# A bank for each strand of side work, and an earlier turn for attention two batches ahead

## The chip, the cores and the metric

The kernel runs on one core of a Trainium2 chip. The metric is the device time of one execution in microseconds. The core's engines are PE (matrix multiply, with a weight load of its own, PEld), DVE (vector), ACT (activation), POOL (GpSimd) and SP, which here only issues DMAs. Each engine works through its own list of instructions in the order in which the program holds them, and semaphores make one engine wait for another.

## The reference, cut to what matters

Eight batches of 576 tokens with 8 heads of 64 go through three layers.

```
q_s = softmax(q, over features); k_s = softmax(k, over tokens)
kv  = k_s^T v             (64 x 64 per head)
x   = q_s kv              -> [8, 576, 512]
u   = x + real(fft over tokens and features of x)
un  = (u - mean) / sqrt(var + 1e-6)
y   = u + relu(un @ w_ch1) @ w_ch2          (512 -> 2048 -> 512)
xk, xr = mixes of y and of y one token earlier
k   = relu(xk @ w_k);  v = (k*k) @ w_v      (512 -> 1024 -> 512)
out = sigmoid(xr @ w_r) * v
```

All of it is float32 in and out. The kernel splits the large operands into two half-precision parts and multiplies three times instead of once.

## The kernel before, in words

The 4608 tokens are worked on in nine blocks of 512, while attention, the transform and their sums go by batches of 576. Block 1 needs all of batch 1 up to token 1023, so its norm needs the transform of batch 1; the norm of block 2 needs the transform of batch 2, and so on.

The feed-forward part (FFN) of a block runs over 16 steps f. `mm1(f)` is 12 matmuls (24 of half width in the first 8 steps of block 0) into one of two banks `h` (L940), then ACT and DVE make `hh` and `hl` of it (L945, L946). `mm2(f)` is 12 matmuls into the four banks `acc0` to `acc3` (L960). PSUM has eight banks: two `h`, four `acc` and two for everything else, the tag `side`.

Beside the FFN of a block runs the side work, in strands written as generators, of which `side()` takes steps at four places of each f. `front_x` is attention for batch after batch: the maxima (L303, L306, L311 to L315), the exponentials (L325, L332), the key-value product (L343, L344) with its scaling (L346 to L354), the transposes of q (L377, L381) emptied by ACT (L370), and the last product (L396) emptied by ACT into `u` (L397). It works in two halves of four heads per batch. `front_y` is the transform of a batch and the norm of the blocks that it completes. The transform forms sums and differences (L430, L441, L446), has a first stage of six groups of matmuls (L475, L478), each emptied by ACT (L482) and DVE (L485), a second stage of five groups (L495 to L499) emptied by L505, L508 and L509, and adds the result to `u` (L511 to L518). The norm makes the mean (L572 and L574 on POOL, L555 on PE, L584) and the variance (L586 and L587 on ACT, L590 and L591 on POOL, L555, L606, L607), a correction (L609 to L612), a product on POOL (L624) and the two halves of the next block's operand (L637 on ACT, L638 on DVE), which the first L940 of that block reads. `front_z` reads and splits the FFN's weights.

While block 0 runs, `side()` gives attention and the transform four turns each as long as attention of batch 1 is undone, then four turns to the transform alone until norm 1 is done. From block 1 on the two alternate.

Each use of a bank by the side work asks `aside` (beside the first batch, where the `acc` banks are free, it takes six banks in turn; later the two `side` banks in turn). A bank is given out again when the last reader of its earlier use is done. The program's order is not the order in which the generators run: a scheduler places the instructions of each engine by when it expects operands and banks to be ready, and then each engine keeps to that list.

After the FFN of block 8 a last part (L1003 to L1054) computes the third layer, with PE busy nearly throughout.

Of the kernel before, what the change touches and what calls it, by code (L numbers as in the profile page):

```python
# [21 lines left out]
NS = 290  # L22
# [21 lines left out]
def net(ctx, tc, q, k, v, w1, w2, mu_k, mu_r, w_k, w_v, w_r, ce_d, se_d, cs_d, ss_d, alt_d, id_d, out):  # L44
# [16 lines left out]

    turn_of = [0]

    def aside(first):

        if not first:
            return bank("side", 2)
        turn_of[0] += 1
        x = turn_of[0] % 6
        return bank("side", 2) if x in (0, 3) else bank(f"acc{(1, 2, 4, 5).index(x)}", 1)  # L70

    mm = nc.tensor.matmul

# [128 lines left out]
    def scales(w):  # L202


        ts = nc.vector.tensor_scalar
        m = wsc[:, 3 * w:3 * w + 1]
        inv = wsc[:, 3 * w + 1:3 * w + 2]
        mi, ii = m.bitcast(U32), inv.bitcast(U32)
        nc.vector.tensor_reduce(out=m, in_=amax[:, w, :], axis=AX.X, op=ALU.add)
        pt = aside(False)[:, 0:1]  # L210
        mm(out=pt, lhsT=one, rhs=m, start=True, stop=True)
        ts(out=inv, in0=pt, scalar1=2.0 ** -120, scalar2=None, op0=ALU.max)
        ts(out=mi, in0=ii, scalar1=1, scalar2=0x3F800000, op0=ALU.logical_shift_right, op1=ALU.bitwise_and)
        ts(out=ii, in0=mi, scalar1=0x7F800000, scalar2=None, op0=ALU.bitwise_xor)

        ts(out=inv, in0=inv, scalar1=(2.0 ** -55, 2.0 ** -51)[w], scalar2=None, op0=ALU.mult)
        ts(out=m, in0=m, scalar1=(2.0 ** 54, 2.0 ** 50)[w], scalar2=None, op0=ALU.mult)
        if w == 1:
            nc.vector.tensor_tensor(out=wsc[:, 6:7], in0=wsc[:, 0:1], in1=m, op=ALU.mult)
# [65 lines left out]
    def attention(b):  # L285
        tt = nc.vector.tensor_tensor
        for hf in range(2):
# [18 lines left out]
                tt(out=m[p, 2 * x:2 * x + 2, :], in0=m[p, 2 * x:2 * x + 2, :], in1=kt[p, 16:18, :], op=ALU.max)  # L306
            if b in MAX_PE:

                pt = aside(b == 0)
                for x in range(2):  # L310
                    nc.tensor.transpose(out=pt[:, 128 * x:128 * x + 128], in_=m[:, 2 * x:2 * x + 2, :], identity=ident)  # L311
                mx = wsc[:, 2:6:3, None]
                nc.vector.tensor_reduce(out=mx[:, :, 0], in_=pt[:, 0:256].rearrange("p (x c) -> p x c", x=2), axis=AX.X, op=ALU.max)
                for x in range(2):
                    mm(out=pt[:, 256 + 128 * x:384 + 128 * x], lhsT=mx[:, x].to_broadcast([128, 128]), rhs=ident, start=True, stop=True)  # L315
                m = pt[:, 256:512].rearrange("p (h d) -> p h d", h=4)
            else:
                nc.gpsimd.partition_all_reduce(out_ap=m, in_ap=m, channels=128, reduce_op=bass_isa.ReduceOp.max)
# [18 lines left out]
            beside = nc.gpsimd.tensor_tensor if (b, hf) in POOL_M else tt  # L337
            beside(out=qt, in0=qt, in1=st[:, 1].to_broadcast([128, 18, 64]), op=ALU.mult)
            yield 0
            kv = aside(b == 0)[:, 0:260].rearrange("p (a e) -> p a e", a=2)  # L340
            for x in range(2):
                for c in range(4):
                    mm(out=kv[:, x, :], lhsT=kc[:, c, 2 * x:2 * x + 2, :], rhs=vt[:, x, c, :], start=(c == 0), stop=False)  # L343
# [28 lines left out]
                    tt(out=dst(qTl), in0=src, in1=dst(qT).bitcast(F32), op=ALU.subtract)  # L372

            for x in range(2):
                pt = aside(b == 0)
                for c in range(4):
                    nc.tensor.transpose(out=pt[:, 128 * c:128 * c + 128], in_=qt[:, 4 * c + 2 * x:4 * c + 2 * x + 2, :], identity=ident)  # L377
                turned(lambda z: z[:, x, 0:512].rearrange("e (p c) -> e c p", c=4), pt.rearrange("e (c p) -> e c p", c=4))
                yield 1
            pt = aside(b == 0)  # L380
            nc.tensor.transpose(out=pt[:, 0:128], in_=qt[:, 16:18, :], identity=ident)  # L381
            turned(lambda z: z[:, :, 512:576], pt[:, 0:128].rearrange("e (x p) -> e x p", x=2))
            if (1, 0) < nxt < (B, 0):
# [5 lines left out]
                U[b] = up.tile([128, 4, S], F32, tag="u", name="u")  # L389
            for x in range(2):  # L390
                for h in range(2):
                    pt = aside(b == 0)
                    hs = slice(HALF * h, HALF * h + HALF)
                    parts = ((bdh, qT), (bdl, qT), (bdh, qTl)) if fx else ((bd, qT),)
                    for z, (a, c) in enumerate(parts):
                        mm(out=pt[:, 0:HALF], lhsT=a[:, x, 0:128], rhs=c[:, x, hs], start=(z == 0), stop=(z == len(parts) - 1))  # L396
                    ma = nc.scalar.activation(out=U[b][:, 2 * hf + x, hs], in_=pt[:, 0:HALF], func=AF.Copy)  # L397
                    if b == 0:
                        mark(hf, mv, ma)
                    yield 1  # L400
# [13 lines left out]
    def transform(b):  # L414
# [52 lines left out]
        for i in range(3):  # L467
            for e, (ch, cl, n0, n1) in enumerate(((ceh, cel, 0, NK), (seh, sel, NK, NK + 256))):
                j0, n = JT[e][i]
                js = slice(j0, j0 + n)  # L470
                pt = aside(b == 0)[0:n, 0:n1 - n0]
                first = True
                for g in range(2):
                    for a, c in ((eh, ch), (eh, cl), (el, ch)):
                        mm(out=pt, lhsT=a[:, e, g, js], rhs=c[:, g, :], start=first, stop=(e == 1 and g == 1 and a is el))  # L475
                        first = False
                if e == 0:
                    mm(out=pt, lhsT=x6[:, js], rhs=alt[:, 0:NK], start=False, stop=True)  # L478
# [10 lines left out]
        sd = fw.tile([128, 2, 2, NS], F32, tag="eo", name="sd")  # L489

        def stage2(cols, ch, cl):
            pt = aside(b == 0)[:, 0:NS]
            for i in range(2):
                for a, c in ((yh, ch), (yh, cl), (yl, ch)):
                    mm(out=pt, lhsT=a[:, i, cols], rhs=c[:, i, :], start=(i == 0 and c is ch and a is yh), stop=False)  # L495
            if ch is csh:
                mm(out=pt, lhsT=yh[0:64, 2, cols], rhs=cl[0:64, 2, :], start=False, stop=False)
            n = 128 if ch is csh else 96
            mm(out=pt, lhsT=yh[0:n, 2, cols], rhs=ch[0:n, 2, :], start=False, stop=True)  # L499
            return pt  # L500
# [49 lines left out]

    def mean(i, sq, cs, n):

        pt = aside(i == 0)
        if i < 2:
            mm(out=pt[:, 0:n], lhsT=ones, rhs=sq[:, 0, cs], start=True, stop=True)  # L555
        else:
            hl = hp.tile([128, 2, 512], F32R, tag="rs", name="hl", bufs=1)
            h, l = hl[:, 0, cs], hl[:, 1, cs]
            nc.scalar.activation(out=h, in_=sq[:, 0, cs], func=AF.Copy)
            nc.vector.tensor_tensor(out=l, in0=sq[:, 0, cs], in1=h.bitcast(F32), op=ALU.subtract)  # L560
            mm(out=pt[:, 0:n], lhsT=onesr, rhs=h, start=True, stop=False)
            mm(out=pt[:, 0:n], lhsT=onesr, rhs=l, start=False, stop=True)
        return pt

    def norm_part(i, sq, d, rs, c0, n):
# [7 lines left out]
        if not onpe:  # L573
            add(out=sq[:, 0, cs], in0=sq[:, 0, cs], in1=sq[:, 1, cs], op=ALU.add)  # L574
            yield 0
            yield 0
            pt = mean(i, sq, cs, n)
        else:
            pt = aside(i == 0)
            for b, s, m, o in segs:  # L580
                for t in range(4):
                    mm(out=pt[:, o - c0:o - c0 + m], lhsT=ones, rhs=U[b][:, t, s:s + m], start=(t == 0), stop=(t == 3))
# [6 lines left out]
        if not onpe:  # L589
            add(out=sq[:, 0:2, cs], in0=sq[:, 0:2, cs], in1=sq[:, 2:4, cs], op=ALU.add)  # L590
            add(out=sq[:, 0, cs], in0=sq[:, 0, cs], in1=sq[:, 1, cs], op=ALU.add)  # L591
            yield 0
            yield 0
            pt = mean(i, sq, cs, n)
        else:
            pt = aside(i == 0)
            for t in range(4):
                mp = mm(out=pt[:, 0:n], lhsT=ones, rhs=sq[:, t, cs], start=(t == 0), stop=(t == 3))
            if i == 0:
                mark(5, mv, ma, mp)  # L600
# [49 lines left out]
    def everywhere(x, n):  # L650

        dg = W["pool"].tile([128, 4, 128], F32, tag="dg", name="dg", bufs=1)[:, 0:n]
        nc.vector.tensor_tensor(out=dg, in0=W["ident"][:, None, :].to_broadcast([128, n, 128]), in1=x[:, :, None].to_broadcast([128, n, 128]), op=ALU.mult)
        pt = bank("side", 2)[:, 0:128 * n]
        mm(out=pt, lhsT=ones, rhs=dg.rearrange("p x c -> p (x c)"), start=True, stop=True)
        nc.vector.tensor_reduce(out=x, in_=pt.rearrange("p (x c) -> p x c", c=128), axis=AX.X, op=ALU.max)
        nc.vector.tensor_scalar(out=x, in0=x, scalar1=float(DM), scalar2=None, op0=ALU.mult)
# [132 lines left out]
    def token_scale(i):  # L790


        n = blocks[i][1]
        pt = bank("side", 2)
        mm(out=pt[:, 0:n], lhsT=W["onesb"], rhs=SQ[i][:, 0:n], start=True, stop=True)
        rg = W["pool"].tile([128, 2, 512], U32, tag="rg", name="rg", bufs=2)
        rb = W["pool"].tile([128, 512], BF16, tag="rb", name="rb", bufs=1)
# [5 lines left out]
    def token_descale(i, rb, subs):  # L803

        z = SC[i][0]
        pt = bank("side", 2)
        for x, (o, m) in enumerate(subs):
            mm(out=pt[0:m, x:x + 1], lhsT=rb[:, o:o + m], rhs=W["onesb"][:, 0:1], start=True, stop=True)
        dd = W["pool"].tile([128, 2, 4], F32, tag="dd", name="dd", bufs=2)
# [358 lines left out]
```

## Time and profile before

| | |
|---|---|
| time, median of 3 runs | 1575.92 us (1575.87 to 1577.27) |
| profiled execution, its own time | 1579.14 us |
| its span, first to last instruction | 1577.2 us |
| granted clock of PE, mean | 0.964 |
| PE busy, share of the span | 93% |
| DVE, ACT, POOL | 59%, 41%, 15% |

A row of a timeline begins with the start in us from the span's start and the duration in us; what follows is the engine, the line of the kernel, the operation, the tile written and the tiles read. In brackets stands how long the engine had been idle and what released it. Matmuls follow each other faster than their duration says, since they are pipelined. A granted clock of 1.00 is 2.4 GHz and one of 0.50 is 1.2 GHz.

### The profile page before, as it was taken

How to read it: one execution, taken by the hardware profiler on the slowest of the kernel's cores; microseconds unless marked ns; L12 is line 12 of the kernel's file. 1: busy time of each engine (PE TensorE's matmuls, PEld its weight loads, DVE VectorE, ACT ScalarE, POOL GpSimd, SP SyncE). 2: the span in 40 equal slices, each digit the busy share in tenths (PEclk: the TensorE clock that was granted, in tenths of full speed). 3: DMA queues.
4: the chain of work that ended last, by engine and by line, in shares of the span. 5: the costliest groups of instructions: out<-in, count | busy, mean ns of one | idle time of the engine just before them, and what ended most of it. 6: DMA issues, size and time to landing. Idle time of an engine off the chain costs nothing. (4 is left out here: it accounts for less than half of the span.)

```text
span 1577.2 us, 18465 instructions
## 1 busy us (share of the span) xinstructions
PE 1459.6 (93%) x7135; PEld 760.4 (48%) x7135; DVE 927.9 (59%) x1629; ACT 651.2 (41%) x1183; POOL 237.9 (15%) x183
## 2 busy tenths in 40 slices
PE   4537998996999999999989989999999999999999
PEld 4425654553555555655545434444444444444444
DVE  7895726648648547556553581686785456554423
ACT  5676513423323233233232441463665445544322
POOL 1663502002010020020010120232010000000000
PEclk9767999997999999999999999999999999999999
DMA  8641102202102102111110540331111011100000
GB/s 308 193 142 47 48 0 75 79 16 74 48 0 74 47 1 74 48 35 43 44 54 1 193 169 1 100 114 64 57 54 54 1 54 54 54 1 27 27 27 27
DMA packets 43988, 99.81 MB, mean 63 GB/s; under 512 B 5723, under 2 KB 12156, under 8 KB 43900
## 3 DMA queue, kind: packets, MB, share of 16 engines
q1 hardware_dynamic: 43900, 98.63, 18.2%
q8 instruction: 56, 0.92, 0.2%
q14 instruction: 32, 0.26, 0.1%
HBM read 79.73 MB, written 18.87 MB: 63 GB/s over the span
## 5 line engine op out<-in xcount | busy, mean ns | idle before, releaser
L940 PE MATMUL h<-unh,wr 128*128 128x512 f16 (+1 forms) x1216 | 378.2, 375 | 38.3 <-ACT unh L637 26.3
L960 PE MATMUL acc<-hh,wr 128*128 128x512 f16 x1152 | 367.0, 381 | 3.9 <-ACT hh L945 3.9
L940 PEld LDWEIGHTS <-wr 128*128 128x128 f16 x1824 | 177.9, 99 | 239.3 <-issue 32.4
L960 PEld LDWEIGHTS <-wr 128*128 128x128 f16 x1728 | 166.3, 98 | 205.4 <-issue 15.1
L940 PE MATMUL h<-unl,wr 128*128 128x512 f16 (+1 forms) x608 | 227.1, 374 | 2.7 <-DVE unl L638 2.5
L960 PE MATMUL acc<-hl,wr 128*128 128x512 f16 x576 | 219.5, 381 | 4.3 <-DVE hl L946 4.3
L946 DVE SCALAR_TENSOR_TENSOR hl<-h,hh 128x512 f16<-128x512 f32 x144 | 98.7, 687 | 161.8 <-ACT hh L945 161.1
L1031 PE MATMUL acc<-wvh,kke 128*128 128x512 f16 x576 | 181.5, 379 | 0.0
L1016 PE MATMUL h<-x,wkh 128*128 128x512 f16 x576 | 171.3, 379 | 0.0
L945 ACT ACTIVATE hh<-h 128x512 f16<-128x512 f32 x144 | 84.5, 590 | 193.0 <-PE h L940 192.9
L1031 PEld LDWEIGHTS <-kke 128*128 128x128 f16 x864 | 84.5, 98 | 102.0
L1021 ACT ACTIVATE kke<-kke 128x512 f32<-128x512 f32 x72 | 45.1, 626 | 164.1 <-DVE kke L1020 164.0
L1020 DVE SCALAR_TENSOR_TENSOR kke<-h,rg 128x512 f32<-128x512 f32 x72 | 49.6, 688 | 102.5 <-PE h L1016 102.4
L1031 PE MATMUL acc<-wvl,kke 128*128 128x512 f16 x288 | 109.2, 379 | 0.0
L1016 PE MATMUL h<-x,wkl 128*128 128x512 f16 x288 | 109.2, 379 | 0.0
L1003 PE MATMUL h<-wrh,x 128*128 128x512 f16 x288 | 88.4, 379 | 1.6 <-ACT kke L1004 1.6
L1016 PEld LDWEIGHTS <-wkh 128*128 128x128 f16 x576 | 55.8, 98 | 66.0
L1023 DVE TENSOR_TENSOR kke<-kke 128x512 f16<-128x512 f32 x72 | 49.6, 689 | 61.0 <-ACT kke L1022 60.5
L572 POOL TENSOR_TENSOR sq<-u 128x128 f32<-128x128 f32 (+7 forms) x15 | 26.4, 1758 | 300.2 <-DVE u L517 133.7
L1003 PEld LDWEIGHTS <-x 128*128 128x128 f16 x432 | 42.3, 98 | 53.3 <-issue 3.0
L780 DVE SCALAR_TENSOR_TENSOR aa<-y,ms,aa 128x512 f32<-128x512 f32 x72 | 62.2, 872 | 4.8 <-ACT aa L776 3.0
L781 ACT ACTIVATE x<-aa 128x512 f16<-128x512 f32 x72 | 44.1, 621 | 35.9 <-PE h L1016 19.0
(322 smaller groups left out, 2170.1 us busy)
## 6 DMA issues: line engine op xcount, KB each, us to landing
vt<-in_v_dram SPq DMA_DIRECT2D x16, 650.0 KB, 5.0
kt<-in_k_dram SPq DMA_DIRECT2D x16, 576.0 KB, 3.8
qt<-in_q_dram SPq DMA_DIRECT2D x16, 576.0 KB, 3.7
out_dram<-oo SPq DMA_DIRECT2D x36, 256.0 KB, 2.1
y<-yT SPq DMA_DIRECT2D x8, 1026.0 KB, 4.9
raw<-in_w_dram SPq DMA_DIRECT2D x16, 512.0 KB, 4.4
words<-in_w_dram SPq DMA_DIRECT2D x16, 512.0 KB, 4.3
raw<-in_w_k_dram SPq DMA_DIRECT2D x32, 256.0 KB, 4.0
```

Source lines behind the costliest of these rows:

```text
L780: nc.vector.scalar_tensor_tensor(out=a, in0=y[:, t, 1:n + 1], scalar=mu[:, w, 0, t:t + 1], in1=a, op0=ALU.mult, op1=ALU.add)
L781: nc.scalar.activation(out=h[:, t, 0:n], in_=a, func=AF.Copy)
L940: mm(out=pt[:, o:o + m], lhsT=a, rhs=c[:, t, o:o + m], start=(t == z == 0), stop=(t == 3 and z == 2))
L945: nc.scalar.activation(out=hh[:, 0:n], in_=pt[:, 0:n], func=AF.Relu)
L946: nc.vector.scalar_tensor_tensor(out=hl[:, 0:n], in0=pt[:, 0:n], scalar=0.0, in1=hh[:, 0:n], op0=ALU.max, op1=ALU.subtract)
L960: mm(out=acc[x][:, 0:n], lhsT=a, rhs=c[:, 0:n], start=(f == z == 0), stop=(f == NF - 1 and z == 2))
L1003: mm(out=pt[0:m, :], lhsT=a[:, t, o:o + m], rhs=c[:, t, :], start=(t == 0 and a is rh and c is wrh), stop=(t == 3 and a is rl))
L1016: mm(out=pt[:, 0:n], lhsT=a[:, t, fs], rhs=c[:, t, 0:n], start=(t == 0 and a is wkh and c is kh), stop=(t == 3 and a is wkl))
L1020: nc.vector.scalar_tensor_tensor(out=kr[:, 0:n], in0=pt[:, 0:n], scalar=0.0, in1=G[:, 0:n], op0=ALU.max, op1=ALU.mult)
L1021: nc.scalar.activation(out=kr[:, 0:n], in_=kr[:, 0:n], func=AF.Square, scale=2.0 ** -76)
L1023: nc.vector.tensor_tensor(out=l2[:, 0:n], in0=kr[:, 0:n], in1=h2[:, 0:n], op=ALU.subtract)
L1031: mm(out=acc[x][0:m, :], lhsT=a[:, o:o + m], rhs=c[:, f, :], start=(f == 0 and a is h2 and c is wvh), stop=(f == NFK - 1 and a is l2))
```

## The change

`aside` takes the strand as a second argument. Strand 0, which is attention and the weights' scale, uses a tag `side0` with one bank; strand 1, which is the transform and the norm, a tag `side1` with one bank. The two banks are the two that `side` had. In the last part the two sums over tokens each get one of the two. And in block 0, once attention of batch 1 is done and until norm 1 is done, attention (of batch 2) gets the third of four turns.

```diff
-    def aside(first):
+    def aside(first, strand):
 
         if not first:
-            return bank("side", 2)
+            return bank(f"side{strand}", 1)
         turn_of[0] += 1
         x = turn_of[0] % 6
-        return bank("side", 2) if x in (0, 3) else bank(f"acc{(1, 2, 4, 5).index(x)}", 1)
+        return bank(f"side{x // 3}", 1) if x in (0, 3) else bank(f"acc{(1, 2, 4, 5).index(x)}", 1)
...
-            kv = aside(b == 0)[:, 0:260].rearrange("p (a e) -> p a e", a=2)
+            kv = aside(b == 0, 0)[:, 0:260].rearrange("p (a e) -> p a e", a=2)
...
-                pt = aside(b == 0)[0:n, 0:n1 - n0]
+                pt = aside(b == 0, 1)[0:n, 0:n1 - n0]
...
-            turns = (sx, sy) * 4 if done_att[0] < 1 else (sy,) * 4 if done_norm[0] < 1 else (sx, sy) * 2
+            turns = (sx, sy) * 4 if done_att[0] < 1 else (sy, sy, sx, sy) if done_norm[0] < 1 else (sx, sy) * 2
```

On PE before, the first group of the first stage of transform 1 stands in the middle of block 0, between FFN matmuls:

```order
L475 MATMUL side<-ceh,eh 128x258
L475 MATMUL side<-cel,eh 128x258
L475 MATMUL side<-ceh,el 128x258
L478 MATMUL side<-alt,x_97 128x258
L940 LDWEIGHTS wr
L940 MATMUL h<-unh,wr 128x512
L960 LDWEIGHTS wr
L960 MATMUL acc_777<-hh,wr 128x512
```

On PE after, the end of the same group, with its numbers of tiles (`side_1053` and `side_1067` are two uses of `side1`), stands at the last FFN matmul of block 0, the L960 here:

```order
L475 MATMUL side_1053<-ceh,el 128x258
L478 MATMUL side_1053<-alt,x_97 128x258
L960 LDWEIGHTS wr
L960 MATMUL acc_780<-hh,wr 128x512
L475 MATMUL side_1067<-seh,eh 128x256
L475 MATMUL side_1067<-sel,eh 128x256
```

What follows it, five groups of the first stage and the whole second stage, moved from the middle of block 0 to behind its end.

The first mean of norm 1 on PE before has FFN matmuls of block 0 on both sides:

```order
L960 LDWEIGHTS wr
L960 MATMUL acc_777<-hh,wr 128x512
L555 MATMUL side<-sq,onesr 128x512
L960 LDWEIGHTS wr
L960 MATMUL acc_777<-hl,wr 128x512
```

The same on PE after, with the variance's L555 six rows later (`kvbd_99` belongs to the second half of a batch, here batch 2):

```order
L396 MATMUL side_1451<-qT,kvbd_99 128x288
L555 MATMUL side_1258<-sq,onesr 128x512
L343 MATMUL side_1528<-vt,kt 128x130 x4
L344 MATMUL side_1528<-vt,kt 128x130
L343 MATMUL side_1528<-vt,kt 128x130 x4
L344 MATMUL side_1528<-vt,kt 128x130
L555 MATMUL side_1280<-sq,onesr 128x512
L377 MATMUL side_1561<-ident,qt 128x128 x4
```

All of this stands after block 0's last FFN matmul and before block 1's first; the last L396 of batch 2 and the key-value product of batch 3 are now around the norm's two products.

On DVE before, from the norm's correction to the first two halves of the operand of block 1:

```order
L609 TENSOR_TENSOR rs<-rs 128x512
L610 SCALAR_TENSOR_TENSOR rs<-side,rs 128x512
L346 TENSOR_SCALAR rk<-side 128x2
L611 TENSOR_SCALAR rs<-rs 128x512
L347 RECIPROCAL rk<-rk 128x2
L612 TENSOR_TENSOR rs<-rs 128x512
L352 TENSOR_TENSOR kvbd_98<-side,rk 64x2x64 x2
L303 TENSOR_REDUCE m<-kt 128x256
L306 TENSOR_TENSOR m<-m,kt 64x128 x2
L638 TENSOR_TENSOR unl<-d,unh 128x512 x2
```

On DVE after, the same place:

```order
L328 TENSOR_TENSOR kt<-kt,m 128x1024
L331 TENSOR_TENSOR kt<-kt,m 64x128 x2
L609 TENSOR_TENSOR rs<-rs 128x512
L610 SCALAR_TENSOR_TENSOR rs<-side_1280,rs 128x512
L611 TENSOR_SCALAR rs<-rs 128x512
L612 TENSOR_TENSOR rs<-rs 128x512
L485 TENSOR_TENSOR yl<-side_1550,yh 128x258
L638 TENSOR_TENSOR unl<-d,unh 128x512
L322 TENSOR_REDUCE st<-qt 128x18
L638 TENSOR_TENSOR unl<-d,unh 128x512
L485 TENSOR_TENSOR yl<-side_1567,yh 128x256
L324 TENSOR_TENSOR qt<-qt,st 128x1152
```

The attention here is that of batch 3 instead of batch 2, and steps of transform 2 stand between the four L638.

## Rows read from the trace of the kernel before

**Rows 1.** The page, busy us, share of the span, instructions of each engine.
```profile
PE 1459.6 (93%) x7135; PEld 760.4 (48%) x7135; DVE 927.9 (59%) x1629; ACT 651.2 (41%) x1183; POOL 237.9 (15%) x183
```
**Rows 2.** The waits of PE: us in total, times, longest us.
```profile
PE h L940 <- ACT unh L637: 26.3, 3, 17.1
```
**Rows 3.** Windows: length, busy us (instructions) by engine, PEclk, DMA share, GB/s.
```profile
119.00:245.40 126.40, 116.54 (x653) 72.77 (x652) 66.21 (x109) 59.17 (x104) 36.72 (x29) 0.93 0.08 31
245.40:258.80 13.40, 7.16 (x38) 4.96 (x38) 6.63 (x12) 5.16 (x9) 8.65 (x5) 0.94 0.58 209
258.80:366.50 107.70, 107.68 (x547) 59.37 (x545) 60.98 (x105) 35.84 (x64) 8.83 (x6) 0.99 0.11 35
366.50:384.40 17.90, 7.92 (x45) 6.70 (x44) 17.03 (x24) 6.48 (x15) 6.76 (x3) 0.69 0.46 163
384.40:394.00 9.60, 7.04 (x17) 2.36 (x17) 9.49 (x13) 4.32 (x7) 1.46 (x2) 0.51 0.00 1
700.00:720.00 20.00, 17.37 (x89) 9.57 (x88) 18.84 (x32) 7.32 (x13) 2.38 (x2) 0.91 0.46 146
816.00:824.00 8.00, 4.33 (x13) 1.87 (x13) 7.91 (x12) 3.65 (x7) 2.53 (x2) 0.57 0.42 142
```
**Rows 4.** Timeline of PE at the starts of blocks 1 and 2.
```profile
249.73 1.06 PE L343 MATMUL side<-vt,kt 128*128 128x130 f32 x8
...
258.83 1.06 PE L940 MATMUL h<-unh,wr 128*128 128x512 f16 x2
...
384.43 1.01 PE L940 MATMUL h<-unh,wr 128*128 128x512 f16 x2 [6.76 <-ACT unh L637]
...
394.04 0.38 PE L940 MATMUL h<-unl,wr 128*128 128x512 f16 x1
394.25 0.59 PE L940 MATMUL h<-unh,wr 128*128 128x512 f16 x2
```
**Rows 5.** Timeline of transform 1 in block 0, its groups and their emptying.
```profile
199.69 0.47 PE L475 MATMUL side<-seh,eh 128*128 128x256 f32 x1
...
201.72 0.39 PE L940 MATMUL h<-unh,wr 128*128 128x512 f16 x1
...
201.82 0.39 ACT L482 ACTIVATE yh<-side 128x258 fp32r<-128x258 f32 x1 [0.65 <-PE side L478]
...
202.24 0.43 DVE L485 TENSOR_TENSOR yl<-side,yh 128x258 fp32r<-128x258 f32 x1 [0.61 <-ACT yh L482]
...
212.86 0.30 PE L495 MATMUL side<-csh,yh 128*128 128x290 f32 x1
...
214.32 0.39 PE L940 MATMUL h<-unh,wr 128*128 128x512 f16 x1
...
218.46 0.48 PE L495 MATMUL side<-ssh,yh 128*128 128x290 f32 x1
...
219.59 0.30 PE L495 MATMUL side<-csh,yh 128*128 128x290 f32 x1
```
**Rows 6.** Timeline of norm 1 and of block 0's end, three engines.
```profile
230.57 0.75 DVE L518 TENSOR_TENSOR u<-u,sd 128x574 f32<-128x574 f32 x1
...
233.55 1.26 POOL L574 TENSOR_TENSOR sq<-sq 128x512 f32<-128x512 f32 x1
...
239.45 1.02 PE L555 MATMUL side<-sq,onesr 128*128 128x512 f32 x2
...
243.53 2.72 DVE L978 SCALAR_TENSOR_TENSOR u<-acc,wsc,u 128x512 f32<-128x512 f32 x4 [0.67 <-PE acc L960]
...
254.00 4.68 POOL L624 TENSOR_TENSOR d<-d,rs 128x1024 f32<-128x1024 f32 x2 [3.29 <-DVE rs L612]
```
**Rows 7.** DVE by line: count, busy us, mean ns, idle before, releaser.
```profile
L303 DVE TENSOR_REDUCE m<-kt 128x256 f32<-128x1024 f32 x16 | 31.0, 1936 | 15.0 <-DMA kt<-in_k_dram 15.0
L334 DVE TENSOR_REDUCE st<-qt 128x18 f32<-128x1152 f32 x16 | 21.6, 1349 | 7.4 <-ACT qt L325 7.4
L328 DVE TENSOR_TENSOR kt<-kt,m 128x1024 f32<-128x1024 f32 x10 | 12.2, 1222 | 1.6 <-POOL m L318 1.6
```

More of the change, by code (lines that the diff above doesn't have):

```diff
@@ L209, in scales @@
         nc.vector.tensor_reduce(out=m, in_=amax[:, w, :], axis=AX.X, op=ALU.add)
-        pt = aside(False)[:, 0:1]
+        pt = aside(False, 0)[:, 0:1]
         mm(out=pt, lhsT=one, rhs=m, start=True, stop=True)
@@ L307, in attention @@
             if b in MAX_PE:
-                pt = aside(b == 0)
+                pt = aside(b == 0, 0)
                 for x in range(2):
@@ L374, in attention @@
             for x in range(2):
-                pt = aside(b == 0)
+                pt = aside(b == 0, 0)
                 for c in range(4):
@@ L379, in attention @@
                 yield 1
-            pt = aside(b == 0)
+            pt = aside(b == 0, 0)
             nc.tensor.transpose(out=pt[:, 0:128], in_=qt[:, 16:18, :], identity=ident)
@@ L391, in attention @@
                 for h in range(2):
-                    pt = aside(b == 0)
+                    pt = aside(b == 0, 0)
                     hs = slice(HALF * h, HALF * h + HALF)
@@ L491, in stage2 @@
         def stage2(cols, ch, cl):
-            pt = aside(b == 0)[:, 0:NS]
+            pt = aside(b == 0, 1)[:, 0:NS]
             for i in range(2):
@@ L551, in mean @@
     def mean(i, sq, cs, n):
-        pt = aside(i == 0)
+        pt = aside(i == 0, 1)
         if i < 2:
@@ L578, in norm_part @@
         else:
-            pt = aside(i == 0)
+            pt = aside(i == 0, 1)
             for b, s, m, o in segs:
@@ L595, in norm_part @@
         else:
-            pt = aside(i == 0)
+            pt = aside(i == 0, 1)
             for t in range(4):
@@ L653, in everywhere @@
         nc.vector.tensor_tensor(out=dg, in0=W["ident"][:, None, :].to_broadcast([128, n, 128]), in1=x[:, :, None].to_broadcast([128, n, 128]), op=ALU.mult)
-        pt = bank("side", 2)[:, 0:128 * n]
+        pt = bank("side0", 1)[:, 0:128 * n]
         mm(out=pt, lhsT=ones, rhs=dg.rearrange("p x c -> p (x c)"), start=True, stop=True)
@@ L793, in token_scale @@
         n = blocks[i][1]
-        pt = bank("side", 2)
+        pt = bank("side0", 1)
         mm(out=pt[:, 0:n], lhsT=W["onesb"], rhs=SQ[i][:, 0:n], start=True, stop=True)
@@ L805, in token_descale @@
         z = SC[i][0]
-        pt = bank("side", 2)
+        pt = bank("side1", 1)
         for x, (o, m) in enumerate(subs):
```

## The prediction

> **What bounds the kernel now.** I read the page first, then the waits of PE, then windows cut at the ends of the feed-forward (FFN) blocks, then the timeline at those ends. The page shows PE busy for 93% of the span [rows 1], so time is lost only where PE stands still or runs at half speed. The waits say where: the largest releaser of PE is L637, the first operand of the next block, three times, 17.1 us of them at the start of block 0 and the rest at later block starts [rows 2]. The windows give the price of the starts [rows 3]. Inside block 0 PE is busy for 116.5 of 126.4 us and inside block 1 for 107.68 of 107.70, although the side work (attention, transform, norm) runs there: beside FFN matmuls it costs PE its own time and no waiting. Between block 0 and block 1, from 245.4 to 258.8, PE is busy for 7.2 of 13.4 us. Between block 1 and block 2 PE is busy for 7.9 of 17.9 us, and then runs 9.6 us at a granted clock of 0.51, the 1.2 GHz level. Two smaller places follow, at 700 to 720 and 816 to 824. So what counts is how much of the norm that a block needs is still undone when the FFN matmuls of the block before run out.
>
> **What the change adds: the transform of batch 1 loses its cover.** The program holds as many instructions on PE, DVE, ACT and SP after as before; all is order. With one bank, every step of attention waits until ACT or DVE has emptied the step before, and the order places these steps some 21 FFN matmuls apart. Attention of batch 1 now ends near the end of block 0 instead of half way. The order shows the consequence. Before, the first stage of transform 1 (L475), its second stage (L495) and the first mean (L555) stood among the FFN matmuls of block 0. After, only the first of six L475 groups does; then block 0's last matmul is issued, and five L475 groups, all of L495 and both L555 follow, with attention of batch 2, half of batch 3 and two groups of transform 2 between them, and no FFN matmul before L940 of block 1, which needs the norm. I work out the length of this uncovered stretch, counted from block 0's last FFN matmul.
>
> First the chain alone. A pair of L475 groups takes 2.03 us on PE (199.69 to 201.72), and the bank is free after L482 (0.39) and L485 (0.43) [rows 5]: with one bank a group costs 1.0 + 0.95, near 2.0 us, and five cost 10. Stage two has csh groups of 1.46 us (212.86 to 214.32) and ssh groups of 1.13 (218.46 to 219.59) [rows 5]; with their evacuation in series, and the four additions to u behind them, I take 12.6. The norm took from the end of L518 (231.3) to the end of the first of two L624, which together are 4.68 (256.3), and 0.6 for L637: 25.6 us, in which L555 stood ready at 234.8 and started at 239.45 [rows 6]: 21.0 without that wait. Before the chain moves, DVE has the four L978, L328 and L331 in front of the first L485: 3. Sum 46.6 us.
>
> Then what stands in the way. DVE is in order, and its list from block 0's last L946 to the first L638 grows from 10 to 59 us when each instruction is priced at its mean: three L303 (1.94 each), three L322 and three L334 (1.35), four L328 (1.22) and the tail [rows 7]. Some 3 us of it are done before the block ends, so 56 is a floor unless instructions overlap. Step by step along the queues I find these delays on the chain: 1.3 for the key-value product of batch 2 (two runs of eight L343 of 1.06 each, with L344 some 2.4 us on PE [rows 4]) in front of the third L475 group; 2.0 for an L303 that waits for its keys (its group waited 15.0 us on that DMA in all [rows 7]) in front of an L485; 1 and 1.4 for L396, L381 and L311 in front of groups; 1.7 to 3.6 for the second key-value product in front of the last ssh group; 1.7 for L370 in front of L515; 2 for L322, L430 and L324 in front of L584; 6 for the 17 us of DVE work between L584 and L609, more than ACT, POOL and PE take there. Sum 17 to 19, so 64 to 65 us. If PE runs at the lower level throughout, its groups take up to twice as long and the sum is 73. Here PE is busy for about half the time, and in 366.5 to 394 it ran at 0.69 and then 0.51 in such a state [rows 3]; I take the middle, 69.
>
> Its end is not clean either: behind the first L638 stand L322, L485 and L324 before the last L638, so the first L940 group ends 3.8 us late, and 1.5 more go in the return to full speed. So 74 us pass. In them PE does useful work that it would have done anyway: transform 1 (5.0 + 6.6), two L555 (2.0), two groups of transform 2 (2.0), and three times what the stretch 245.4 to 258.8 holds without its L555 (7.16 - 1.0, at full speed near 5.8, [rows 3]), with 0.4 for L311 and L315: 33. **Added: 74 - 33 = 41 us.** Bounds: 56 with the same tail, less 33, is 27; 73 and 9 more for DVE slowed beside POOL is 54.
>
> The Trainium skill has a rule against this change: "Perfetto Trace Analysis", Matmuls, says that independent groups should rotate through several banks, so that emptying one overlaps the next group's matmuls. The trace agrees in the price of a handover, 0.95 us behind a group [rows 5], and by that rule alone eleven groups of transform 1 would lose some 10 us; in the sum above these are in the 10 and the 12.6.
>
> The skill's "TensorE: Matmul & The Clock Gate", HAM oscillation, says that waits between bursts of matmuls throttle PE and the next burst starts slow. The rows 366.5 to 394 agree [rows 3]; by it the stretch would be 73 and the added part 45, without it 64 and 36.
>
> **What the change removes.** The old gap between block 0 and 1: 13.4 us with 6.1 us of useful work at full speed, and 1.3 in a slow start: 8.6 [rows 3, 4]. The gap between block 1 and 2: from 366.5 to 394.0 only 19 FFN matmuls were done (4.1 us at the spacing of 394.04 to 394.25) and side work that is busy for 7.9, some 6.1 at full speed: 17.3 [rows 3, 4]. It goes, since norm 2 stands in block 1's first half after the change (its last L562 halfway through, before the last L562 stood behind block 1's matmuls). What is late next there is nothing that I see: L624 of norm 2 is issued some three f steps early. The two later places are 3.5 and 5.2 us [rows 3]; norm 6 moves ahead of its block's end in the order, the other place I cannot tell: 5 of 8.7. **Removed: 8.6 + 17.3 + 5 = 31 us**, bounds 26 and 37 (all of 8.7, and 2.5 for a wait in block 0). The rest costs nothing: after block 5 both orders have the same norms at the same rows, and the tail is PE bound.
>
> Sum: 41 - 31 = **10 us slower**; 1589 against the profiled execution's 1579.1 (span 1577.2 and 1.9 around it), and 1586 against the median of 1575.9, which lies 3.2 lower. A measurement of this kernel tells 0.2%, 3.2 us, from no change. From the bounds: 27 - 37 = -10 to 54 - 26 = +28, so 1566 to 1604.
>
> **Rivals.**
> *The head start wins.* The stretch is bound by DVE's list alone and that is shorter than its means: four L978 in a row took 2.72 [rows 6], where four means of 0.744 make 2.98, and at that ratio the list of 56 comes to 51. Then 51 + 3.8 - 33 = 22 is added, 37 removed: -15, 1561. For it: PE and ACT work there is interleaved just so that the banks alternate, and block 1 starts with attention 2 done. Against: the chain has waits for keys and two PE queues in it. It decides from a stretch under some 56 us to L940, or under 62 if all 37 are removed.
> *The single bank stalls PE inside the blocks too.* PE is in order; where a bank is not emptied when the next side group is due, FFN matmuls wait behind it. After block 0 attention makes about 130 handovers; at 0.2 us each that is 26, 1612. For it: nothing can overtake on PE. Against: the order puts 4.5 us of FFN between handovers, and PE stood busy through block 1 [rows 3].
> *It comes out even*, within 3 us: a stretch of 56 to 62 us with 31 removed, or the bank split does nothing, as there are two side banks before and after. Against the latter: the order, in which the split doubles the length of attention 1.
>
> **Chances.** Forecast, +3 to +28: 0.58. Stalls in the blocks, or a stretch over 82: 0.10. Even: 0.08. Head start wins: 0.24. So slower 0.68, same 0.08, faster 0.24. The forecast's own range is 1579 to 1604; with 0.03 left out above and the reach into the faster side, 1564 to 1607.
>
> **What would show it.** In the profile after: a stretch of 60 to 80 us with no L940 or L960 near 232 to 305, PE about half busy at a clock of 0.5 to 0.8 in it; L940 released by L637 or L638 at its end; no gap of over 3 us between blocks 1 and 2; PE without waits inside block 1. If block 1 starts before 290, or L377 and L396 wait inside blocks, or the gap between block 1 and 2 stays, a step is wrong.

## The result

The changed kernel takes 1597.37 us (median; 1595.03 to 1597.77), the kernel before 1576.16 in the same comparison: +21.2 us, a ratio of 1.0130 [1.0114, 1.0146]. The forecast was +10. The profiled execution of after is the fastest of its runs (1595.03, span 1593.2), that of before the slowest of its own (1579.14): between the two traces 16.0 us of span are to be explained.

The page and the waits of PE after, which answer to [rows 1, 2]:

```profile
PE 1465.1 (92%) x7135; PEld 762.8 (48%) x7135; DVE 932.9 (59%) x1629; ACT 654.2 (41%) x1183; POOL 237.2 (15%) x183
```
```profile
PE h L940 <- ACT unh L637: 16.5, 2, 14.1
PE h L940 <- DVE hl L946: 11.3, 10, 3.0
...
PE side L555 <- POOL sq L574: 6.4, 1, 6.4
PE side L561 <- ACT hl L559: 6.3, 1, 6.3
...
PE side L555 <- POOL sq L591: 5.3, 1, 5.3
PE h L940 <- DVE unl L638: 5.0, 2, 3.8
```

The waits for L637, 26.3 us in three before, are 16.5 in two. The three waits for the norm's own middle, L555 twice and L561 once, come to 18.0 us; before, one of them was there:

```profile
PE side L555 <- POOL sq L591: 3.3, 1, 3.3
```

The windows of after (columns as in [rows 3]), cut at its own block ends, show where they lie:

```profile
119.00:227.20 108.20, 102.36 (x578) 62.55 (x576) 53.01 (x90) 50.59 (x87) 32.17 (x25) 0.92 0.11 38
227.20:304.60 77.40, 45.91 (x200) 32.00 (x200) 47.80 (x88) 28.72 (x49) 13.53 (x9) 0.73 0.23 81
304.60:425.10 120.50, 113.00 (x561) 61.77 (x561) 75.27 (x109) 40.10 (x71) 18.49 (x11) 0.95 0.10 34
425.10:529.60 104.50, 104.50 (x542) 57.78 (x540) 61.40 (x94) 35.12 (x63) 10.14 (x8) 1.00 0.12 43
```

Block 0 ends at 227.2 (before 245.4), and then come 77.4 us without an L940 or L960. Block 2 begins at 425.1 (before 384.4). In block 1 PE now stands still for 7.5 us, where it ran without a pause from 258.8 to 366.5 before; the pause between blocks 1 and 2 is gone.

I count as **lost** the time in which PE is idle, and half of its busy time at 1.2 GHz (from the granted clock, piece by piece). Span less lost is PE's work at full speed: 1426.0 us before and 1427.9 after. Lost is 151.2 before and 165.3 after:

| stretch | before | after |
|---|---|---|
| up to block 0, and block 0 | 80.1 + 16.8 | 74.7 + 15.8 |
| block 0's last FFN matmul to block 1 | 7.0 | 44.1 |
| block 1 with the gap behind it, block 2 | 12.6 + 5.9 | 12.1 + 0 |
| blocks 3 to 8 | 23.5 | 13.3 |
| last part | 5.3 | 5.3 |

What held up the norms stands in the timeline of after, several engines:

```profile
263.22 1.52 POOL L318 PARTITION_ALL_REDUCE m<-m  x1 [54.42 <-DVE m L306]
263.71 1.17 DVE L518 TENSOR_TENSOR u<-u,sd 128x574 f32<-128x574 f32 x1
272.42 2.06 POOL L572 TENSOR_TENSOR sq<-u 128x896 f32<-128x896 f32 x1 [7.67 <-DVE qt L324]
...
275.87 2.07 PE L555 MATMUL side<-sq,onesr 128*128 128x512 f32 x2 [6.45 <-POOL sq L574]
...
284.93 1.26 POOL L591 TENSOR_TENSOR sq<-sq 128x512 f32<-128x512 f32 x1
292.13 1.34 POOL L318 PARTITION_ALL_REDUCE m<-m  x1 [5.94 <-issue]
...
297.17 0.69 DVE L612 TENSOR_TENSOR rs<-rs 128x512 f32<-128x512 f32 x1
300.85 0.71 POOL L572 TENSOR_TENSOR sq<-u 128x256 f32<-128x256 f32 x1 [7.38 <-issue]
301.54 4.64 POOL L624 TENSOR_TENSOR d<-d,rs 128x1024 f32<-128x1024 f32 x2
...
378.23 1.09 POOL L318 PARTITION_ALL_REDUCE m<-m  x1 [8.49 <-DVE m L306]
386.41 2.33 POOL L590 TENSOR_TENSOR sq<-sq 128x1024 f32<-128x1024 f32 x1 [7.10 <-issue]
...
390.11 0.63 ACT L559 ACTIVATE hl<-sq 128x512 fp32r<-128x512 f32 x1 [6.78 <-POOL sq L591]
390.79 0.79 PE L561 MATMUL side<-hl,onesr 128*128 128x512 f32 x1 [6.32 <-ACT hl L559]
```

The sum of transform 1 is complete at 264.9 (L518), but L572, which only reads it, starts at 272.4: POOL had run L318, the maximum of batch 3, until 264.7. The label of 272.42 names L324, but L324 is no operand of L572. What stands between is not in a timeline, which leaves out what the queue of an engine does by itself, but in the view of the line (instructions, shortest, median and longest ns, first and last start in us):

```profile
L572 POOLq MODIFY_POOL_CONFIG  x2: 98/98/98, 264.7 to 264.7; - x2
L572 POOLq EVENT_SEMAPHORE  x1: 17/17/17, 264.9 to 264.9; - x1
L572 POOL TENSOR_TENSOR sq<-u x1: 2063/2063/2063, 272.4 to 272.4; 128x896 f32<-128x896 f32 x1
```

As soon as L318 is over, POOL's queue holds a pair of MODIFY_POOL_CONFIG. The wait for the sum is met at 264.9, and L572 starts 7.5 us later. Such a pair stands wherever POOL goes from an all-reduce to a tensor operation or back, and in the four places shown where the operand was there before the pause was over, POOL ran nothing for 5.9 to 7.7 us; L624 behind L572 needs no pair and starts at once. Where the operand comes later, nothing is lost: the pair ahead of the L318 of 263.22 stands at 208.8, and that L318 starts 0.2 us after its operand. Three of the four changes lie beside the chain of norm 1, the one at 386 on that of norm 2. Beside the blocks the changed kernel makes 16 of them and the kernel before 10 (pairs at L572 and L590 one way, at L318 the other); the whole lines of L318, before and after:

```profile
L318 POOLq MODIFY_POOL_CONFIG  x10: 4/8/11, 258.6 to 701.3; - x10
L318 POOLq MODIFY_POOL_CONFIG  x16: 1/1/11, 208.8 to 709.1; - x16
```

### The profile page after: what moved, and what is told of

Same layout as the page of the kernel before. It is cut to its first block, busy times and chain, and to the rows that moved or that the text cites. A ratio compares the mean times of both kernels' runs of the same rounds, so it can differ in the third digit from the quotient of the medians.

```text
span 1593.2 us, 18482 instructions
## 1 busy us (share of the span) xinstructions
PE 1465.1 (92%) x7135; PEld 762.8 (48%) x7135; DVE 932.9 (59%) x1629; ACT 654.2 (41%) x1183; POOL 237.2 (15%) x183
## 4 chain that ended last, share of the span: by engine, by line
PE 75%; DVE 14%; ACT 4%; DMA 4%; issue 2%; POOL 1%; SPq 0%; ACTq 0%; POOLq 0%; DVEq 0%
PE h L940 20%; PE acc L960 19%; PE h L1016 12%; PE acc L1031 9%; PE h L1003 4%; PE side L475 2%; PE side L343 2%; PE side L495 2%; PE side L396 1%; DVE wr L194 1%; DMA raw<-in_w_v_dram 1%; DVE aa L780 1%; DVE wr L193 1%; DMA raw<-in_w_k_dram 1%; DVE d L624 1%
## 5 line engine op out<-in xcount | busy, mean ns | idle before, releaser
L940 PE MATMUL h<-unh,wr 128*128 128x512 f16 (+1 forms) x1216 | 377.1, 373 | 33.3 <-ACT unh L637 16.5
L960 PE MATMUL acc<-hh,wr 128*128 128x512 f16 x1152 | 367.6, 380 | 0.0
L940 PEld LDWEIGHTS <-wr 128*128 128x128 f16 x1824 | 177.0, 99 | 233.9 <-issue 33.5
L960 PEld LDWEIGHTS <-wr 128*128 128x128 f16 x1728 | 165.5, 98 | 191.1 <-issue 4.4
L940 PE MATMUL h<-unl,wr 128*128 128x512 f16 (+1 forms) x608 | 226.5, 373 | 5.0 <-DVE unl L638 5.0
L960 PE MATMUL acc<-hl,wr 128*128 128x512 f16 x576 | 218.8, 380 | 0.3 <-DVE hl L946 0.3
L946 DVE SCALAR_TENSOR_TENSOR hl<-h,hh 128x512 f16<-128x512 f32 x144 | 98.9, 687 | 167.9 <-ACT hh L945 167.2
L1020 DVE SCALAR_TENSOR_TENSOR kke<-h,rg 128x512 f32<-128x512 f32 x72 | 49.6, 688 | 103.0 <-PE h L1016 102.7
L1023 DVE TENSOR_TENSOR kke<-kke 128x512 f16<-128x512 f32 x72 | 49.6, 689 | 60.7 <-ACT kke L1022 60.3
L786 POOL TENSOR_TENSOR s<-s 128x1024 f32<-128x1024 f32 x9 | 21.2, 2354 | 267.4 <-ACT s L784 217.1
L572 POOL TENSOR_TENSOR sq<-u 128x128 f32<-128x128 f32 (+7 forms) x15 | 24.5, 1630 | 228.9 <-DVE u L517 97.0
```

What stands on the lines that cost most here:

```text
L940: mm(out=pt[:, o:o + m], lhsT=a, rhs=c[:, t, o:o + m], start=(t == z == 0), stop=(t == 3 and z == 2))
L946: nc.vector.scalar_tensor_tensor(out=hl[:, 0:n], in0=pt[:, 0:n], scalar=0.0, in1=hh[:, 0:n], op0=ALU.max, op1=ALU.subtract)
L960: mm(out=acc[x][:, 0:n], lhsT=a, rhs=c[:, 0:n], start=(f == z == 0), stop=(f == NF - 1 and z == 2))
L1020: nc.vector.scalar_tensor_tensor(out=kr[:, 0:n], in0=pt[:, 0:n], scalar=0.0, in1=G[:, 0:n], op0=ALU.max, op1=ALU.mult)
L1023: nc.vector.tensor_tensor(out=l2[:, 0:n], in0=kr[:, 0:n], in1=h2[:, 0:n], op=ALU.subtract)
```

## The experiments

Theory A, the forecast's: the bank split slows attention 1, and transform 1 loses its cover. Theory B: the turns given to batch three push norm 1 back. Theory C, formed on the trace above: POOL's changes between L318 and ordinary operations make up what the forecast missed. The ratios stand against the kernel before in the same comparison; "stretch" runs from block 0's last FFN matmul to block 1; work is span less lost.

| kernel | stretch | block 2 at | lost | work | ratio [95%] |
|---|---|---|---|---|---|
| before | 13.4 | 384.4 | 151.2 | 1426.0 | 1 |
| changed | 77.4 | 425.1 | 165.3 | 1427.9 | 1.0130 [1.0114, 1.0146] |
| split alone | 77.0 | 424.8 | 163.4 | 1428.1 | 1.0108 [1.0090, 1.0127] |
| turns alone | 27.2 | 382.0 | 159.6 | 1427.1 | 1.0049 [1.0035, 1.0063] |
| changed, max of 3 on PE | 66.1 | 412.8 | 159.1 | 1430.9 | 1.0068 [1.0045, 1.0092] |
| changed, max of 3 and 4 on PE | 66.2 | 406.4 | 148.3 | 1433.1 | 1.0019 [1.0005, 1.0032] |
| changed, all max on PE | 64.6 | 401.4 | 175.5 | 1436.0 | 1.0228 [1.0212, 1.0244] |
| before, all max on PE | 13.5 | 383.9 | 159.7 | 1435.7 | 1.0136 [1.0117, 1.0154] |
| banks in turn, attention 1 | 27.6 | 400.1 | 143.9 | 1428.5 | 0.9961 [0.9948, 0.9974] |
| in turn from the 7th | 49.6 | 400.8 | 145.8 | 1427.2 | 0.9984 [0.9973, 0.9995] |
| the same, max of 3 on PE | 43.9 | 403.4 | 147.5 | 1430.2 | 1.0012 [1.0002, 1.0022] |
| the same, max of 3 and 4 on PE | 42.7 | 390.7 | 147.4 | 1431.2 | 1.0023 [1.0013, 1.0032] |
| the same, all max on PE | 43.7 | 390.0 | 176.7 | 1435.4 | 1.0238 [1.0217, 1.0258] |
| in turn, attention 1, all max on PE | 26.8 | 388.8 | 189.1 | 1438.3 | 1.0323 [1.0306, 1.0340] |

### The two parts of the change

The split alone (the changed kernel with the old turns):

```diff
-turns = (sx, sy) * 4 if done_att[0] < 1 else (sy, sy, sx, sy) if done_norm[0] < 1 else (sx, sy) * 2
+turns = (sx, sy) * 4 if done_att[0] < 1 else (sy,) * 4 if done_norm[0] < 1 else (sx, sy) * 2
```


> The split of the banks alone: attention's steps and the transform's each keep one bank, the turns beside block 0 are those of before. In its order the same things stand behind block 0's last FFN matmul as in the changed kernel (five L475 groups, all L495, both L555), only shuffled among themselves. Theory A, the bank split makes the uncovered stretch: within 5 us of the changed kernel, +16 to +26 us against before, and again some 75 to 80 us without L940 or L960. Theory B, the turns given to batch three push norm 1 back: the stretch falls to some 20 us and the time to 1570 to 1580.

Its window of the stretch is that of the changed kernel:

```profile
227.10:304.10 77.00, 46.24 (x200) 32.31 (x200) 48.36 (x88) 28.74 (x49) 14.38 (x9) 0.71 0.24 81
```

PE is busy for 46.2 of 77.0 us, against 45.9 of 77.4. Theory A holds: the split alone makes the stretch and at least most of the loss. The intervals of the two ratios overlap, so these runs do not settle whether the turns add anything to the split.

The turns alone is the kernel before with the changed kernel's line of turns (the + and - above swapped).

> The turns alone, with two banks that all side work shares in turn as before. Its order has the transform of batch 1 among the FFN matmuls of block 0 and norm 2's last L562 a hundred FFN matmuls before the end of block 1 (before, it stood behind them). Theory A: no stretch of over 20 us between blocks 0 and 1, and the gap between blocks 1 and 2 shrinks from 27 us lost or slow to under 10: 1560 to 1572. Theory B: +10 to +25 us against before, with a stretch as long as in the changed kernel. Theory C, POOL's change from L318 to ordinary operations (some 7 us each time) costs wherever the all-reduce of batch 3 lies beside norm 1 or 2: a stall of about 6 us of L555 or L561 stays and the gain is under 5 us.

Its windows, and what PE waited for in the first of them:

```profile
247.80:275.00 27.20, 11.71 (x39) 7.89 (x39) 14.73 (x23) 7.68 (x12) 9.34 (x5) 0.56 0.08 31
275.00:382.00 107.00, 107.00 (x550) 59.41 (x549) 59.25 (x99) 38.02 (x67) 14.67 (x9) 1.00 0.16 52
```
```profile
PE side L555 <- POOL sq L591: 8.6, 1, 8.6
PE side L343 <- ACT kt L332: 5.1, 1, 5.1
```

This missed: theory A's 1560 to 1572 was 14 us or more too low. With shared banks theory B is half right: the gap in front of block 1 grows from 13.4 to 27.2, as the first L555 stands at the end of block 0 and the second behind its last FFN matmul, and batch 3's key-value product (L343) gets in front of L940. The gap behind block 1 goes here too: PE is busy in all of 275 to 382. So either part of the change removes it by itself. Theory C is not what made L555 wait here: in that trace POOL's L590 waited 11.4 us for ACT's L587, without a change on POOL.

### The change of operation on POOL

```diff
-MAX_PE = (0, 1, 2)
+MAX_PE = (0, 1, 2, 3)
```


> The changed kernel with the maximum of batch 3 taken on PE (L311 and L315) in place of POOL's L318, so that no L318 stands beside norms 1 and 2. The same transform groups stand uncovered behind block 0 as in the changed kernel. Theory C, that POOL's changes between L318 and ordinary operations cost about 7 us each on the norm's chain: L555 waits 0 to 2 us in place of 6.45 and 5.27, the 6.3 us wait of L561 inside block 1 goes with its slow clock, the stretch is 62 to 68 us in place of 77, and the time 10 to 18 us under the changed kernel (1579 to 1587). Without it (the waits come from what is queued on DVE and ACT): within 4 us of the changed kernel.

The waits of PE in the stretch no longer have L555 in them, and the stretch is 66.1 instead of 77.4:

```profile
PE side L315 <- DVE wsc L313: 4.8, 1, 4.8
PE side L343 <- ACT kt L332: 4.2, 1, 4.2
```

From 1.0130 to 1.0068 is 9.8 us, just under what theory C forecast, and the wait of L561, which it forecast to go, stayed with 3.9 us: the next L318, of batch 4, had moved in front of norm 2's squares. POOL there, and then PE's L561:

```profile
345.26 1.52 POOL L318 PARTITION_ALL_REDUCE m<-m  x1 [50.56 <-DVE m L306]
353.50 1.79 POOL L572 TENSOR_TENSOR sq<-u 128x768 f32<-128x768 f32 x1 [6.72 <-issue]
...
357.34 0.79 PE L561 MATMUL side<-hl,onesr 128*128 128x512 f32 x1 [3.92 <-ACT hl L559]
```

The same with `MAX_PE = (0, 1, 2, 3, 4)`:

> The changed kernel with the maximum of batches 3 and 4 on PE, those of 5 to 7 stay on POOL. The kernel with all on PE reached block 2 at 401.4 us, 23.7 earlier than the changed kernel, and lost it again from block 3 on, with 12.5 and 6.4 us of waits around norm 6 at 938 to 953. If the early gain is POOL's change beside norms 1 and 2, and the later loss comes from taking the maxima of batches 5 to 7 on PE: block 2 at 400 to 403, then the changed kernel's 1168 us from there to the end, 1570 to 1578. If the later loss comes from being ahead (attention of later batches runs into the norms): 1590 to 1612.

```profile
227.60:293.80 66.20, 45.13 (x201) 33.14 (x202) 48.08 (x83) 26.67 (x47) 12.45 (x7) 0.74 0.24 83
293.80:406.40 112.60, 111.21 (x558) 61.73 (x558) 66.08 (x101) 37.73 (x67) 15.26 (x9) 0.97 0.11 35
```
```profile
266.40 2.28 POOL L572 TENSOR_TENSOR sq<-u 128x896 f32<-128x896 f32 x1 [57.24 <-DVE u L518]
268.76 1.37 POOL L574 TENSOR_TENSOR sq<-sq 128x512 f32<-128x512 f32 x1
...
290.59 4.71 POOL L624 TENSOR_TENSOR d<-d,rs 128x1024 f32<-128x1024 f32 x2 [2.85 <-DVE rk L347]
```

Here L572 is released by the sum itself, and the wait of L561 in block 1 is gone. The lost time falls by 17.0 us, of which 11.3 in the stretch and 7.4 in block 1; PE has 5.2 us more work. The ratio falls from 1.0130 to 1.0019, though less than expected: block 2 at 406.4 and 1580.7 us miss the 400 to 403 and 1570 to 1578. Theory C is shown for these two norms: with the same transform uncovered, but without POOL's changes beside them, the kernel is 0.2% above before. The stretch still loses 32.8 us, but the gaps that the change removes outweigh that.

With every maximum on PE:

> The changed kernel with the maximum of every batch on PE, so that POOL runs no L318 at all. The uncovered work behind block 0 is the same as in the changed kernel. If POOL's changes are what made the stretch and the second gap longer than forecast: a stretch of 62 to 68 us as in the kernel that took only batch 3 off POOL, no wait of L561 inside blocks 1 and 2 (in that kernel one of 3.9 us and one of 4.1 us beside the remaining L318), 1576 to 1583. If the waits only move: 1586 to 1592, as with batch 3 alone.

Block 2 starts at 401.4, as in the expectation, but the kernel is slower than the changed one. Its waits of PE from 836 to 953:

```profile
PE h L940 <- ACT unh L637: 12.5, 1, 12.5
PE side L561 <- ACT hl L559: 6.4, 1, 6.4
```

These are norm 7, the norm of the block that starts at 952.6 (the expectation above calls it norm 6). With the maxima of batches 5 to 7 back on POOL they are absent, so it is these three that bring them. The sum that norm 7 needs is late there: its L572 starts 81 us after block 6 does, against 45 us with only 3 and 4 on PE. Why the three push it back I did not follow, and the 1576 to 1583 was missed by 31 us.

> The kernel before with the maximum of every batch on PE. Its order keeps norm 2 at the very end of block 1 (L561 at 1704 and 1728 of 1728 FFN matmuls), so the gap between blocks 1 and 2 should stay or grow. If POOL's changes cost as much before as after, 1568 to 1574; if they matter only where norm and all-reduce meet, as the theory has it, within 5 us of before, since in the kernel before no L318 lies between the squares of norm 1 or 2.

This missed too: +21 us. PE's work grows by 9.7 us for five batches, and 8.5 us more are lost in all: 13 more in blocks 3 to 8, and less elsewhere. A maximum on PE is no free exchange.

### Attention 1 with two banks

```diff
     turn_of = [0]
+    alt_of = [0]
 
     def aside(first, strand):
 
+        if not first and done_att[0] < 1:
+            alt_of[0] += 1
+            return bank(f"side{alt_of[0] % 2}", 1)
         if not first:
             return bank(f"side{strand}", 1)
```


> The changed kernel, but until attention of batch 1 is done each side step takes the two banks in turn, whichever strand it belongs to; from then on one bank per strand. In its order attention 1 ends after 310 of block 0's 960 FFN matmuls (in the changed kernel after 872), the six L475 groups stand at 444 to 690, L495 at 736 to 870 and the first L555 at 950. Theory A (attention 1 with one bank is what takes the cover away): the stretch falls to 15 to 30 us and the time is 30 to 45 us under the changed kernel, 1552 to 1567. If one bank for the transform or the norm itself is what costs: the stretch stays over 50 us and the time within 10 us of the changed kernel.

```profile
130.90:259.30 128.40, 120.11 (x685) 75.91 (x686) 75.95 (x114) 59.64 (x105) 36.31 (x28) 0.93 0.13 47
259.30:286.90 27.60, 15.38 (x47) 9.39 (x46) 22.11 (x38) 11.94 (x22) 11.26 (x6) 0.65 0.30 106
```

The stretch falls from 77.4 to 27.6 us. That confirms theory A by the one edit that undoes its cause. "Perfetto Trace Analysis", Matmuls, of the Trainium skill says that independent groups should rotate through several banks, and the two stretches agree with it for attention 1. It is the fastest kernel run here, 0.9961 [0.9948, 0.9974]. The expectation of 1552 to 1567 was too low (1572.2): block 0 starts at 130.9 instead of 114.2, since attention 1's first steps now stand in front of it.

To keep those steps behind the start, the rotation begins with the seventh handover (`if alt_of[0] > 6`). Without any other edit:

> The banks in turn for attention of batch 1 from the seventh handover on, with the maxima where the changed kernel has them (batches 0 to 2 on PE). In its order POOL finishes norm 1 (L572 to L624) before the next L318, and the squares of norm 2 too; one L318 pair stands ahead of norm 2's L624. Each batch whose maximum is on PE adds some 2 to 3 us of PE work (span less idle and slow time: 1428 for the changed kernel, 1433 with two batches more, 1436 with five more), which is not paid here. Cover without PE's extra work: a stretch of 40 to 48 us, no wait of L561 in block 1, 1562 to 1572, faster than both kernels. If the L318 ahead of L624 delays norm 2, block 2 starts with a gap of 3 to 7 us and the time is 1570 to 1578.

With the maximum of batch 3 on PE, then of 3 and 4, then of all; and last, all on PE with the rotation from the start:

> The same with the maximum of batch 3 alone on PE: one L318 of batch 4 stands beside norm 2 in block 1 again. Theory C: a wait of L561 of 4 to 7 us in the second half of block 1, block 2 at 394 to 402, and 1562 to 1576.

> The banks in turn for attention of batch 1 from the seventh handover on, and the maximum of batches 3 and 4 on PE. As in the kernel with all maxima on PE, block 2 should start at 390 (a stretch of 43 us behind block 0). With the later blocks of the changed kernel (1168 us from there): 1558 to 1566, faster than both kernels. If being ahead is what costs later: 1590 to 1610.

> As the kernel without any L318, and attention of batch 1 takes the banks in turn from its seventh handover on, so that its first half group beside the start stays as in the changed kernel. In its order all L475 groups of transform 1 stand inside block 0 (640 to 854 of 960) and two of five L495 groups; three L495 groups and both L555 are behind the last matmul. Theory A: each group put under cover takes about 2 us off the stretch, five L475 and two L495 groups and what stands between them some 20 to 25: a stretch of 38 to 48 us, block 0 starting at 113 to 116, and 1556 to 1566.

> As the kernel that takes the banks in turn for attention of batch 1, with the maximum of every batch on PE. All of transform 1 is covered. Theory A with the switch: a stretch of 18 to 28 us, block 0 starting at about 125 to 131 since attention 1's first steps stand before it, no wait of L555 or L561 over 2 us: 1560 to 1570. It would beat both kernels if the later blocks stay without gaps.

Of these five expectations one held in time, and by luck. Rotation from the seventh takes 1574.5 us, 0.9984 [0.9973, 0.9995], inside its second range, but block 2 starts without the gap that was to bring it there. My reading of its order was wrong: an L318 does stand between the squares of norm 1, and L595 (the changed kernel's L590, five lines lower here) follows it after 7.88 us; the stretch is 49.6, above the 40 to 48. The other four missed: 1579.4 against 1562 to 1576, 1581.5 against 1558 to 1566 or 1590 to 1610, 1615.0 against 1556 to 1566, and 1629.0 against 1560 to 1570. With batch 3 on PE the L318 of batch 4 does the same between two squares of norm 2, and PE waits 9.2 us:

```profile
346.55 1.81 POOL L577 TENSOR_TENSOR sq<-u 128x768 f32<-128x768 f32 x1 [59.89 <-DVE u L523]
354.25 1.08 POOL L323 PARTITION_ALL_REDUCE m<-m  x1 [5.89 <-PE h L945]
362.31 1.25 POOL L579 TENSOR_TENSOR sq<-sq 128x512 f32<-128x512 f32 x1 [6.98 <-issue]
```
```profile
PE side L566 <- ACT hl L564: 9.2, 1, 9.2
```

The pair of kernels with the maxima of 3 and 4 on PE tells what cover is worth. The stretch shrinks from 66.2 to 42.7, block 2 starts 15.7 us earlier, and the ratios are the same (1.0019, 1.0023). Blocks 3 and 4 of the kernel that is ahead:

```profile
495.80:610.80 115.00, 112.11 (x596) 64.28 (x595) 80.38 (x123) 42.54 (x74) 11.72 (x10) 1.00 0.16 56
610.80:723.80 113.00, 111.15 (x561) 61.30 (x561) 78.52 (x117) 39.13 (x70) 12.54 (x9) 0.97 0.14 45
```

They take 115.0 and 113.0 us where the other kernel has 106.2 and 107.9, partly because side work moved there (112.1 of PE against 106.2), partly because 7.4 us are lost, against 0.2. A shorter stretch counts only by the lost time in it, here 25.3 against 32.8, and that was lost again later. The last two kernels lose late, as all with every maximum on PE do, and for them too the cause is open.

## Why the prediction was right in direction and short by half

**The step that failed** is the list of what stands in the way of a norm. It was made from the queues of PE, DVE and ACT, and POOL's changes between L318 and tensor operations stand in it at nothing; the count of instructions, the same before and after, was of PE, DVE, ACT and SP, and left out POOL, whose queue holds 12 more MODIFY_POOL_CONFIG after. The runs show them in two terms of the sum: 11.3 us in the stretch behind block 0 and 8.7 us at norm 2 in block 1.

**Added, 41.** Measured 77.4 us to the first L940, of which 33.3 are useful work at full speed: 44.1. To this point the forecast had 69 less 33, that is 36; its 5 for an unclean end lie behind the first L940, where 3.4 were lost (1.2 idle, 2.2 at the lower clock). So 47.5 stand against 41. The mechanism, the five uncovered L475 groups and the useful part were right. Without POOL's changes the same stretch is 66.2 and loses 32.8, so the rest of the chain was 3 us shorter than forecast, and that hides part of the 11.3 that are missing from the list of delays. The clock was half right: PE was not at 1.2 GHz throughout but from 262 to 279 and 286 to 310 and in two short pieces, 0.73 on the mean, where the two stretches between blocks 1 and 2 before have 0.69 and 0.51 [rows 3]; 12.6 us were lost by it. The sums with PE at that level throughout (73) and not at all (64 to 65) hold the 66.2 between them. "TensorE: Matmul & The Clock Gate", HAM oscillation, of the Trainium skill says that waits between bursts throttle PE, and the 0.73 agrees; by it alone the stretch would have been the 73.

**Removed, 8.6 between block 0 and 1.** 7.0 by the lost time, and 0.9 of the slow start, which the table has in block 1.

**Removed, 17.3 between block 1 and 2.** "It goes, since norm 2 stands in block 1's first half", and "What is late next there is nothing that I see." The gap went, but L561 of norm 2 was late next, 6.32 us two thirds through block 1, and behind it PE ran at 1.2 GHz for some 5 us: 8.7 lost. Lost in blocks 1 and 2: 18.5 before, 12.1 after, so 6.4 removed (9.8 without the 3.4 of the unclean end). With no L318 beside norm 2 the loss in block 1 is 4.7 with the maxima of 3 and 4 on PE, all of it the unclean end, and 1.1 with all on PE. I had looked at the PE order of norm 2 and at DVE's and ACT's lists, and not at POOL's, where an L318 stands between L574 and L590. POOL was 15% busy [rows 1], which says nothing about an engine that pauses between its instructions.

**Removed, 5 at the two later places.** By the lost time they were 4.3 and 5.7 us, not 3.5 and 5.2. The lost time of blocks 3 to 8 fell by 10.2: both places went, and smaller waits of PE for L946 came (11.3 in ten, where before had 4.9 in five).

**Not foreseen:** block 0 and its start lose 6.4 us less, and PE's work is 1.9 more. The terms then are 44.1 - 7.0 - 6.4 - 10.2 - 6.4 + 1.9 = 16.0, the difference of the spans. The medians differ by 5 us more, since the two profiled executions lie 2.3 and 3.0 from their medians towards each other. That the sum came as near as it did is luck in part: the 20 us of POOL's changes were set off by the 6.4 here, by 5 more at the later places and by the shorter chain.

**The signs named ahead.** The stretch of 60 to 80 us near 232 to 305 came (227.2 to 304.6); PE in it was busy for 59% at a clock of 0.73; L940 was released by L637 and L638; no gap lies between blocks 1 and 2. "PE without waits inside block 1" failed, and that was the sign of the wrong step. Of the rivals, the head start that wins did not come, since the stretch is 77; stalls of the single bank inside blocks did not come either: what stalled PE in block 1 was POOL, not a bank.

## What to carry to other kernels

Before a change is priced that brings two strands closer together, list what each shared in-order engine runs in turn, the rarely used one too, and look in the trace for pauses between kinds of instructions, not only at busy shares. As long as one strand stands in front of what the next block needs, as attention 1 did, give it two banks in turn; in the fastest kernel here each strand keeps one from then on. And count moved side work by the lost time it removes: time that a block gains by doing work elsewhere comes back where that work is done.

## What the runs showed of the hardware

When POOL goes from the all-reduce across partitions (L318) to a tensor operation, or back, its queue holds a pair of MODIFY_POOL_CONFIG at the end of the earlier one, and in none of the fourteen traces does the next start earlier than some 5.6 us (to the all-reduce) or 6.7 us (to a tensor operation) behind the start of the pair. Where the next was ready, POOL stood idle: 7.67, 5.94, 7.38 and 7.10 us after, and 6.72 and 6.98 in two of the experiments. Where its operand came later than that, the pair cost nothing; between tensor operations that are ready there is no pause. A MEMSET (L457) behind an all-reduce has no pair in the trace of before, and at 391.21 it starts at once. That trace already held one pause, unseen, since its label names a DVE instruction and no norm stood behind it:

```profile
382.13 2.11 POOL L572 TENSOR_TENSOR sq<-u 128x384 f32<-128x384 f32 x1
390.08 1.25 POOL L318 PARTITION_ALL_REDUCE m<-m  x1 [5.84 <-DVE qt L324]
```

"GPSIMD Engine Reference", Instruction dispatch, of the Trainium skill says that the first call to a freshly loaded kernel pays about 6 us with no instruction to be seen in the profile, counted from MODIFY_POOL_CONFIG. The rows agree in kind and size. What they add is that this program has such a pair, and so the price, at every change between the two kinds, in both directions.
